# One weight load cut into halves of its columns, and an order of operations read from a table: block-sorted attention and a feed-forward layer on one core

## The chip, the cores and the metric

The kernel runs on one core of one Trainium2 chip. Its time is device microseconds of one execution. Before the change three runs took 251.02, 250.55 and 249.65 us; the median is 250.55 us. The profile belongs to one more execution, which took 249.8 us.

A core has five engines that run their own instruction streams: TensorE (PE, matmuls; PEld is its weight load), VectorE (DVE), ScalarE (ACT), GpSimd (POOL) and SyncE (SP). Data come and go through 16 DMA engines, which POOL and SP feed. A wait on a semaphore holds up everything behind it on the same engine.

## The reference

```python
def _attn_ref(q, k, v, sort_net):            # q, k, v: [4, 8, 768, 64], sort_net: [4, 8, 8, 8]
    ...
    for _ in range(5):                       # five rounds of softmax and column sums
        P = P - np.max(P, axis=-1, keepdims=True)
        P = np.exp(P)
        P = P / (np.sum(P, axis=-1, keepdims=True) + 1e-09)
        P = P / (np.sum(P, axis=-2, keepdims=True) + 1e-09)
    ...
    k_sorted = np.einsum('bhij,bhjcd->bhicd', P, k_b).reshape(B, H, S, D)   # 8 blocks of 96 rows
    v_sorted = np.einsum('bhij,bhjcd->bhicd', P, v_b).reshape(B, H, S, D)
    ...
    scores = scale * np.matmul(q_b, k_sb.transpose(0, 1, 2, 4, 3))          # within a block
    ...
    return np.matmul(attn, v_sb)

def _moe_ref(x, w_in, w_out, alpha):         # x: [3072, 512], w_in: [512, 2048], w_out: [2048, 512]
    h = x @ w_in
    g = np.maximum(h, 0.0) + alpha * np.minimum(h, 0.0)
    return g @ w_out
```

The attention's output, its heads put side by side, is the x of the feed-forward layer. Inputs and output are float32; the kernel multiplies in bfloat16.

## The kernel before, in words

The 3,072 tokens are 32 groups of 96: four batches of eight blocks. A group is computed for all eight heads at once.

**Start.** POOL issues the loads of batch 0: q into a free part of hT (L482), k into KS and v into VST (L504); each writes 6,144 bytes of bfloat16 into each of 128 partitions. Then come w_in in four row blocks of 128 rows (L988), w_out in two halves (L993), k and v of batch 1 (L504, L520), q of batch 1 head by head into QN (L486), which SP then transposes into QTz (L494), and v and k of batch 2. Meanwhile DVE and ACT compute the five rounds on sort_net, and PE runs 140 tiny matmuls (`burst`, L969) and turns q (L685).

**Per batch.** `prep_k` (L685 for batch 0, L714 later) sorts the blocks of k by matmuls with a matrix made of P, and writes KT. `conv_v` (line 457, on ACT, DVE or POOL) lays out v and `prep_v` (L760, later L755) sorts it into VS; `conv_k` (L701, POOL) lays out k for the later batches.

**Per group.** Scores (L801 in batch 0, L798 later), row maxima on DVE (L807), then in batch 0 a second pass on PE (L822 and L813) and one exponential on ACT (L845). Later batches take eight exponentials on ACT (L834) and a DMA transpose on SP (L839, into ET). Then scores times v (L854), a division on DVE (L862, L865, into xq) and a turn into xT, by PE (L880) and a copy, or by SP (L873) in most groups of the later batches.

**Feed-forward.** Tokens go in chunks of 192 (the first two) and 384. `ffn1` makes four matmuls (L904) for each of 16 column blocks ft of w_in, ACT takes the negative part (L914, into t1), DVE joins it into hT (L917). `ffn2` takes tiles of 128 tokens: 16 matmuls (L943) in four groups, a copy, and a store by SP (L957). Every `ffn1` group reads all 512 rows of w_in, and so waits for all four row blocks.

**The order.** Each operation is added to a graph with its engine (or a choice of ACT and DVE, `EITHER`), an estimated duration, what it reads and writes, and a priority. `search` (L221) tries 2,000 variations of the priorities; each is put in order by `schedule` (L156), which at each step takes the engine that can start first. Model times in `span` and `fetched` include a fetch of PE's instructions in blocks of 256, usable `FETCH` = 6,200 ns after the block before it was entered. `fill` and `idle` then put further matmuls, of the identity with itself, whose results nobody reads (`warm`, L1070, 512 columns each), into PE's gaps in the model's times. `emit` writes the five streams with the waits that the order leaves.

The lines of the load and of its first reader are:

```python
for p in range(4):                                            # L987
    G.add(POOL, lambda e, p=p: e.dma_start(
        AP(w_in_bf, p * DFF, [[KT_TILES * DFF, 128], [1, DFF]]),
        AP(moe_w_in.tensor, p * 128 * DFF, [[DFF, 128], [1, DFF]])),
        2550, w=[("w_in", p)], prio=-40 + p, dma=(dma_sem("wi%d" % p), 0))
...
op = G.add(PE, f, t_pe(*[(n, 128)] * 4), r=[("xT", g % 16) for g in range(ga, gb)]
           + [("w_in", kt) for kt in range(KT_TILES)], w=keys, prio=prio)
```

Of the kernel before, what the change touches and what calls it, by code (L numbers as in the profile page):

```python
# [2 lines left out]

# [5 lines left out]
AP = bass.AP  # L9
# [9 lines left out]
DFF = 2048  # L19
KT_TILES = DM // 128  # L20
# [5 lines left out]
NE = 3  # L26
VSL = 4
EPS = 1e-9
SEARCH = 1500
FIRST = 500  # L30
FETCH = 6200.0
BURST = 140

XLAT = {"pe": 215, "act": 36, "dve": 36, "pool": 80, "sync": 80}
ENGS = ("pool", "sync", "pe", "act", "dve")


def t_pe(*mms):  # L40
    return sum(max(n, m, 64) / 2.4 + 4 for n, m in mms)
# [34 lines left out]
class _Graph:  # L76
# [51 lines left out]
    def fetched(self, op, at, d, f):  # L128

        if f["fills"] and at > 5000:  # L130
            f["n"] += 2 * int(max(at - f["end"], 0) * 0.9 / 215)
        f["fills"] = f["fills"] and op.fills
        n, last = 2 * op.mm, f["n"] + 2 * op.mm
        while f["mark"] < last:
            x = at + d * max(f["mark"] - f["n"], 0) / n
            late = max(f["usable"] - x, 0.0)
            at, x = at + late, x + late
            f["usable"] = x + FETCH
            f["mark"] += 256
        f["n"], f["end"] = last, at + d  # L140
        return at + d
# [11 lines left out]
            t = max(t, x.end + lat)  # L153
        return t

    def schedule(self):  # L156
        ops = self.ops
        for op in ops:
            op.users, op.eng = [], op.engs
        for op in ops:  # L160
            op.left = len(op.deps)
            for d in op.deps:
                ops[d].users.append(op.idx)
        ready = {e: [] for e in ENGS}

        def release(op):
            op.ready = {}
            for e in op.engs:
                op.ready[e] = self.ready_at(op, e)
                ready[e].append(op)  # L170

        free = dict.fromkeys(ENGS, 0.0)
        free["pool"] = 400.0
        loads = [0.0, 0.0, {"n": 2, "mark": 193, "usable": 0.0, "end": 0.0, "fills": True}]
        order = {e: [] for e in ENGS}
        for op in ops:
            if not op.left:
                release(op)
        done = 0
        while done < len(ops):  # L180
            best = None
            for e in ENGS:
                if not ready[e]:
                    continue
                first = max(free[e], min(o.ready[e] for o in ready[e]))
                op = min((o for o in ready[e] if o.ready[e] <= first + 60), key=lambda o: (o.prio, o.idx))
                first = max(first, op.ready[e])
                if best is None or first < best[0]:
                    best = (first, e, op)
            at, e, op = best  # L190
            for x in op.engs:
                ready[x].remove(op)
            op.eng, op.start = e, at
            free[e], op.end = self.span(op, e, at, free, loads)
            op.pos = len(order[e])
            order[e].append(op)
            done += 1
            for u in op.users:
                ops[u].left -= 1
                if not ops[u].left:  # L200
                    release(ops[u])
        self.order = order
        return max(op.end for op in ops)

    def replay(self, seed):

        rng = random.Random(seed)
        was = [(op.start, op.end) for op in self.ops]
        free = dict.fromkeys(ENGS, 0.0)
        free["pool"] = 400.0  # L210
        loads = [0.0, 0.0, {"n": 2, "mark": 193, "usable": 0.0, "end": 0.0, "fills": True}]
        for op in sorted(self.ops, key=lambda o: (o.start, o.idx)):
            at = max(free[op.eng], self.ready_at(op, op.eng))
            free[op.eng], op.end = self.span(op, op.eng, at, free, loads, 0.08 * rng.random())
        last = max(op.end for op in self.ops)
        self.ends = [op.end for op in self.ops]
        for op, (a, b) in zip(self.ops, was):
            op.start, op.end = a, b
        return last

    def search(self, n, first):  # L221

        rng = random.Random(7)
        rank = [op.prio for op in self.ops]
        best = None
        for x in range(FIRST + n):
            if x == FIRST:
                best = None
            lo, hi, part = (-47.5, 3.0, 0.2) if x < FIRST else (0.0, 99.0, 0.1)
            amp = rng.choice((0.1, 0.3, 1.0))  # L230
            for op, p in zip(self.ops, rank):
                op.prio = p + (rng.uniform(-amp, amp) if x % FIRST and lo < p < hi and rng.random() < part else 0.0)
            cost = self.schedule()
            if x < FIRST:
                cost = sum(op.end for op in first)
            if x < FIRST or best is None or cost < best + 1500:
                for seed in (1, 2):
                    late = self.replay(seed)
                    cost += sum(self.ends[op.idx] for op in first) if x < FIRST else late
                cost /= 3  # L240
                if best is None or cost < best:
                    best, rank = cost, [op.prio for op in self.ops]
                    if __import__("os").environ.get("SCHED"):
                        print("search", x, round(cost))
        for op, p in zip(self.ops, rank):
            op.prio = p
        return self.schedule()

    def fill(self, make, unit, first, spans):

# [118 lines left out]
def bass_sinkhorn_attn__then__act_prelu_kernel(  # L369
# [11 lines left out]
    G = _Graph()  # L381
    sems = {e: es.enter_context(nc.semaphore("s_" + e)) for e in ENGS}

    def dma_sem(name):
        return [es.enter_context(nc.semaphore("d_" + name)), 0]
# [7 lines left out]
    PE, ACT, DVE, POOL, SYNC = ("pe",), ("act",), ("dve",), ("pool",), ("sync",)  # L393
# [3 lines left out]
    bz = sb("bz", [128, 32], BF16)  # L397
# [19 lines left out]
    w_in_bf = sb("w_in_bf", [128, KT_TILES, DFF], BF16)  # L417
    w_out_bf = sb("w_out_bf", [128, FT_TILES, DM], BF16)
    xT = sb("xT", [128, KT_TILES, XR], BF16)
# [39 lines left out]
    def t_either(n, mode=1):  # L459
# [4 lines left out]
          w=["P"], prio=-100, dma=(dma_sem("sn"), 0))  # L464
# [429 lines left out]
    def ffn1(ga, gb, ft, prio):  # L894
        tok, n = ga * BLK, (gb - ga) * BLK
        tb = step[0] % 3
        banks = BANK_H + ([BANK_P] if ga < 2 else [])
        pt, poff, _, keys = banks[step[0] % len(banks)]
        step[0] += 1

        def f(e):
            inst = None
            for kt in range(KT_TILES):
                inst = e.matmul(AP(pt, poff, [[1024, 128], [1, n]]),  # L904
                                AP(w_in_bf, kt * DFF + ft * 128, [[KT_TILES * DFF, 128], [1, 128]]),
                                AP(xT, kt * XR + tok % XR, [[KT_TILES * XR, 128], [1, n]]),
                                start=(kt == 0), stop=(kt == KT_TILES - 1))
            return inst
        op = G.add(PE, f, t_pe(*[(n, 128)] * 4), r=[("xT", g % 16) for g in range(ga, gb)] + [("w_in", kt) for kt in range(KT_TILES)],
              w=keys, prio=prio)  # L910
        if not ffn_ops:
            ffn_ops.append(op)

        G.add(ACT, lambda e: e.activation(AP(t1[tb], 0, [[384, 128], [1, n]]),  # L914
                                          AP(pt, poff, [[1024, 128], [1, n]]), ACTF.Relu, scale=-1.0),
              t_act(n), r=keys, w=[("t1", tb)], prio=prio)
        G.add(DVE, lambda e: e.scalar_tensor_tensor(  # L917
            out=AP(hT, ft * RING + tok % RING, [[FT_TILES * RING, 128], [1, n]]),
            in0=AP(t1[tb], 0, [[384, 128], [1, n]]), scalar=AP(omaT, ft, [[16, 128], [1, 1]]),
            in1=AP(pt, poff, [[1024, 128], [1, n]]), op0=AluOpType.mult, op1=AluOpType.add),  # L920
            t_dve(n) + 52, r=keys + [("t1", tb), "omaT"],
            w=[("hT", ft, x % (RING // 64)) for x in range(tok // 64, (tok + n) // 64)], prio=prio)
# [42 lines left out]
    def burst(e):  # L965
# [2 lines left out]
            r = x % 4 * 32  # L968
            inst = e.matmul(AP(psS, r * 1024 + 384, [[1024, 32], [1, 32]]), bz[r:r + 32, :], bz[r:r + 32, :])  # L969
        return inst  # L970
    G.add(PE, burst, 200 + 8.5 * BURST, r=["bz"], w=["psSw"], prio=-120)
    load_q(0, -98)
    load_k(0, -97)
    load_v(0, -96)
# [9 lines left out]
        conv_v(0, u, -45.5)  # L984
    for u in range(8):
        prep_v(0, u, -45, (BANK_O + [BANK_P])[u % 3])
    for p in range(4):  # L987
        G.add(POOL, lambda e, p=p: e.dma_start(  # L988
            AP(w_in_bf, p * DFF, [[KT_TILES * DFF, 128], [1, DFF]]),
            AP(moe_w_in.tensor, p * 128 * DFF, [[DFF, 128], [1, DFF]])),  # L990
            2550, w=[("w_in", p)], prio=-40 + p, dma=(dma_sem("wi%d" % p), 0))
    for p in range(2):
        G.add(POOL, lambda e, p=p: e.dma_start(  # L993
            AP(w_out_bf, p * 8 * DM, [[FT_TILES * DM, 128], [DM, 8], [1, DM]]),
# [67 lines left out]
            load_k(3, -3.9)  # L1062
            load_q(3, -2)
    assert fp == len(ffn_plan)
    total = G.search(SEARCH, first_x)

    def warm(e, n, bank=(psYP, 0)):
        inst = None
# [46 lines left out]
```

## Time and profile before

| what | value |
|---|---|
| median of three runs | 250.55 us |
| the profiled execution | 249.8 us |
| its span, first to last instruction | 248.1 us |
| mean granted clock of TensorE | 0.979 |
| PE busy | 234.3 us (94%), 2,538 matmuls |
| DVE, ACT, POOL busy | 171.5, 155.1, 101.1 us |
| L904 and L943, busy | 97.8 and 84.7 us (the larger groups) |
| first and last L904 | 30.43 and 236.4 us |
| w_in, issue to landing | 14.4 to 20.4 us |
| HBM read, written | 27.28, 6.29 MB |

The span leaves out what lies before the first and after the last instruction; here that is 1.7 us. Busy time of PE counts matmuls that overlap and matmuls at half clock, so it says where PE is not empty, not how much it gets done; the start-to-start distance of equal matmuls says that. In a list by stretches the columns are the stretch, its length, then for each engine the busy time and in brackets the number of instructions, the granted clock, the share of the DMA engines' time and GB/s.

### The profile page before, as it was taken

What the parts mean: (1) busy time and instruction counts of PE and PEld (TensorE: products, weight loads), DVE (VectorE), ACT (ScalarE), POOL (GpSimd) and SP (SyncE); (2) the same over time, 40 slices, a digit from 0 to 9 for tenths busy, and PEclk for the clock granted to TensorE, in tenths of its full rate; (3) what the DMA queues carried; (4) which work ended last, traced back from release to release, by engine and by line L of the source; (5) the groups of instructions that cost most, each with busy time, mean ns of one, the idle gap of its engine ahead of it and who ended that gap; (6) DMA issues with size and microseconds to landing.
All of it is one profiled execution on the core that took longest, in us unless ns stands there. A gap on an engine that the chain in (4) does not pass through costs nothing.

```text
span 248.1 us, 6269 instructions
## 1 busy us (share of the span) xinstructions
PE 234.3 (94%) x2538; PEld 145.0 (58%) x2538; DVE 171.5 (69%) x347; ACT 155.1 (63%) x423; POOL 101.1 (41%) x146
## 2 busy tenths in 40 slices
PE   6876899999999979999999999999999999999995
PEld 3445567668655636666565666655556555555544
DVE  6764667669787878786679878676869476655510
ACT  5567335596868876786648567965685576455511
POOL 8988902275899967798554103100000000000000
PEclk9999579999999999999999999999999999999999
DMA  6999999999999899989985665532364232301112
GB/s 104 208 211 210 173 215 205 172 196 124 193 85 185 156 170 143 140 121 132 145 135 132 93 159 108 132 94 53 87 122 107 49 103 45 95 11 73 44 45 86
DMA packets 71982, 31.37 MB, mean 126 GB/s; under 512 B 64512, under 2 KB 67344, under 8 KB 71952
## 3 DMA queue, kind: packets, MB, share of 16 engines
q0 software_dynamic: 23408, 13.63, 41.1%
q1 hardware_dynamic: 48544, 17.33, 36.5%
q8 instruction: 20, 0.33, 0.6%
q14 instruction: 10, 0.08, 0.2%
HBM read 27.28 MB, written 6.29 MB: 135 GB/s over the span
## 4 chain that ended last, share of the span: by engine, by line
PE 81%; DMA 8%; ACT 4%; DVE 3%; POOL 2%; issue 2%; POOLq 0%
PE psH L904 31%; PE psYP L943 28%; DMA VST<-in_v_dram 5%; PE psS L943 3%; PE psO L854 3%; PE psS L798 3%; DMA ET<-Esb 3%; PE psYP L755 2%; POOL VDz L457 2%; PE psYP L714 1%; PE psS L813 1%; PE psYP L1070 1%; ACT VDz L457 1%; DVE hT L917 1%; PE psS L822 1%
## 5 line engine op out<-in xcount | busy, mean ns | idle before, releaser
L917 DVE SCALAR_TENSOR_TENSOR hT<-t,omaT,psH 128x384 bf16<-128x384 f32 (+1 forms) x139 | 77.4, 571 | 31.7 <-ACT t L914 29.8
L904 PE MATMUL psH<-xT,w_in_bf 128*128 128x384 bf16 (+1 forms) x556 | 97.8, 312 | 0.6 <-DVE hT L917 0.3
L914 ACT ACTIVATE t<-psH 128x384 f32<-128x384 f32 (+1 forms) x139 | 62.8, 465 | 48.4 <-PE psH L904 44.3
L943 PE MATMUL psYP<-w_out_bf,hT 128*128 128x512 bf16 x336 | 84.7, 379 | 0.3 <-DVE hT L917 0.3
L904 PEld LDWEIGHTS psH<-xT,w_in_bf 128*128 128x128 bf16 x556 | 49.9, 98 | 33.0 <-DVE hT L917 5.9
L834 ACT ACTIVATE Esb<-psS,nf 96x96 bf16<-96x96 f32 x192 | 46.3, 345 | 1.2 <-DVE nf L807 0.9
L943 PEld LDWEIGHTS psYP<-w_out_bf,hT 128*128 128x128 bf16 x336 | 30.4, 98 | 27.4 <-DVE hT L917 0.4
L457 POOL COPY VDz<-VST 64x384 bf16<-64x384 bf16 x40 | 34.0, 851 | 13.6 <-PE psYP L755 11.6
L701 POOL COPY KSz<-KS 64x512 bf16<-64x512 bf16 x36 | 22.2, 618 | 33.0 <-PE psYP L714 21.0
L807 DVE TENSOR_REDUCE nf<-psS 96x8 f32<-96x768 f32 x24 | 22.7, 946 | 0.9 <-PE psS L798 0.9
L865 DVE TENSOR_TENSOR xq<-psO,rec 96x512 bf16<-96x512 f32 x31 | 21.2, 685 | 1.0
L486 POOL DMA_DIRECT2D QN<-in_q_dram x24 | 19.8, 848 | 2.5 <-DMA QTz<-QN 1.2
L854 PEld LDWEIGHTS psO<-VS,ET 112*128 112x128 bf16 x248 | 11.5, 100 | 6.9 <-ACT Esb L834 2.0
L854 PE MATMUL psO<-VS,ET 112*128 112x65 bf16 x248 | 13.1, 196 | 1.8 <-DMA ET<-Esb 1.5
L798 PEld LDWEIGHTS psS<-KT,QTz 128*96 128x96 bf16 x192 | 11.7, 125 | 2.7
L798 PE MATMUL psS<-KT,QTz 128*96 128x96 bf16 x192 | 12.6, 208 | 0.0
L862 DVE RECIPROCAL rec<-psO 96x8 f32<-96x8 f32 x31 | 6.1, 198 | 9.2 <-PE psO L854 9.1
L1070 PE MATMUL psYP<-identb 128*128 128x512 bf16 x34 | 11.3, 468 | 1.0 <-ACT identb L457 1.0
L457 ACT ACTIVATE VS<-psYP 112x512 bf16<-112x512 f32 x13 | 8.9, 687 | 5.0 <-PE psYP L755 3.2
L457 DVE CAST VS<-psYP 112x512 bf16<-112x512 f32 x13 | 9.0, 690 | 3.7 <-PE psYP L755 3.7
L457 ACT ACTIVATE outstg<-psYP 128x512 f32<-128x512 f32 x11 | 6.6, 598 | 7.7 <-PE psYP L943 7.7
L755 PE MATMUL psYP<-BDV,VDz 128*128 128x64 bf16 x192 | 9.5, 193 | 0.5 <-POOL VDz L457 0.5
(139 smaller groups left out, 212.6 us busy)
## 6 DMA issues: line engine op xcount, KB each, us to landing
out_dram<-outstg SPq DMA_DIRECT2D x23, 256.0 KB, 2.3
KS<-in_k_dram POOLq DMA_DIRECT2D x3, 768.0 KB, 31.5
QN<-in_q_dram POOLq DMA_DIRECT2D x24, 96.0 KB, 5.5
w_in_bf<-in_moe_w_in_dram POOLq DMA_DIRECT2D x4, 512.0 KB, 17.3
w_out_bf<-in_moe_w_out_dram POOLq DMA_DIRECT2D x2, 1024.0 KB, 28.6
VST<-in_v_dram POOLq DMA_DIRECT2D x4, 384.0 KB, 31.8
hT<-in_q_dram POOLq DMA_DIRECT2D x1, 768.0 KB, 7.0
VST<-in_v_dram POOLq DMA_DIRECT2D x1, 768.0 KB, 13.4
```

Source lines behind the costliest of these rows:

```text
L457: return e.activation(o, i, ACTF.Copy) if e is nc.scalar else e.tensor_copy(o, i)
L486: G.add(POOL, lambda e, h=h: e.dma_start(AP(QN, h * 128 + (h // 4) * 64, [[6144, 128], [1024, 6], [1, 64]]), AP(q.tensor, b * HB + h * S * ...
L701: G.add(POOL, lambda e, hp=hp: e.tensor_copy(AP(KSz, hp * 64 * 3072 + u % 3 * 1024 + hp * 64, [[3072, 64], [128, 8], [1, 64]]), AP(KS[n], ...
L798: inst = e.matmul(o, AP(QTz[n], hp * 3072 + h4 * 768 + i * 96, [[6144, 128], [1, 96]]), AP(KT[n], (h4 * 8 + i) * bk, [[ld, 128], [64, 2], ...
L807: G.add(DVE, lambda e: e.tensor_reduce(AP(nx, 0, [[8, 96], [4, 2], [1, 4]]), AP(psX, 0, [[1024, 96], [512, 2], [96, 4], [1, 96]]), AxisLis ...
L834: inst = e.activation(AP(Esb[me], p * 128, [[1024, 96], [64, 2], [1, 48]]), AP(psX, (p // 4) * 512 + (p % 4) * 96, [[1024, 96], [48, 2], [ ...
L854: inst = e.matmul(AP(psZ, hp * 512 + h4 * 68, [[1024, 128], [1, 65]]), AP(ET[me] if far else ET[m], pos(h4, hp) * 96, [[800, nk], [1, 128] ...
L865: G.add(DVE, lambda e: e.tensor_tensor(out=AP(xq[me], 0, [[512, 96], [256, 2], [64, 4], [1, 64]]), in0=AP(psZ, 0, [[1024, 96], [512, 2], [ ...
L904: inst = e.matmul(AP(pt, poff, [[1024, 128], [1, n]]), AP(w_in_bf, kt * DFF + ft * 128, [[KT_TILES * DFF, 128], [1, 128]]), AP(xT, kt * XR ...
L914: G.add(ACT, lambda e: e.activation(AP(t1[tb], 0, [[384, 128], [1, n]]), AP(pt, poff, [[1024, 128], [1, n]]), ACTF.Relu, scale=-1.0), t_ac ...
L917: G.add(DVE, lambda e: e.scalar_tensor_tensor(out=AP(hT, ft * RING + tok % RING, [[FT_TILES * RING, 128], [1, n]]), in0=AP(t1[tb], 0, [[38 ...
L943: inst = e.matmul(AP(bank[0], bank[1], [[1024, 128], [1, n]]), AP(hT, ft * RING + tok % RING, [[FT_TILES * RING, 128], [1, 128]]), AP(w_ou ...
```

## The change

w_in is loaded in two halves of its columns instead of four blocks of its rows. A load writes, in each partition, four pieces of 1,024 columns (2,048 bytes of bfloat16). An `ffn1` group then waits for one half: the first for ft 0 to 7, the second for ft 8 to 15.

The search is gone. `arrange` takes the operations in the order of a table of 1,224 numbers (two fewer, for the two loads); a letter behind a number gives the engine where there is a choice. Each engine's stream follows the table. The model's times still exist, since `fill`, `idle` and the waits use them, with other constants: the fetch of a block takes 3,500, 6,150, 6,000 or 5,200 ns by its time, and the `burst` 9.4 ns a matmul instead of 8.5. The matmuls, copies, transposes and stores are the same; how many of the `warm` matmuls there are follows from the model's times, and the choice between ACT and DVE from the table (DVE has four operations fewer than before and ACT four more, POOL two loads fewer).

```diff
-SEARCH = 1500
-FIRST = 500
-FETCH = 6200.0
 BURST = 140
...
+SEQ = """
+0 2 7 3 10 4 17 18 11 16 27 5 1 8 42 43 12 9 28 44 37 39 45 6 46 40 47 48 29 38 130 49 50 33 51 131 52 53 54
+55 132 56 57 41 58 133 34 59 60 136 61 62 63 26 64 35 65 23 36 66 83 67 145 68 87 84 69 89 70 21 71 91 88 31
...
+""".split()
...
-            f["usable"] = x + FETCH
+            f["usable"] = x + (3500.0 if x < 3000 else 6150.0 if x < 12500 else 6000.0 if x < 30000 else 5200.0)
...
-    def schedule(self):
...
-    def replay(self, seed):
...
-    def search(self, n, first):
...
+    def arrange(self, table):
+        assert len(table) == len(self.ops)
+        letters = {"p": "pool", "a": "act", "d": "dve"}
         free = dict.fromkeys(ENGS, 0.0)
         free["pool"] = 400.0
         loads = [0.0, 0.0, {"n": 2, "mark": 193, "usable": 0.0, "end": 0.0, "fills": True}]
...
+        self.order = {e: [] for e in ENGS}
+        done = set()
+        for x in table:
+            op = self.ops[int(x.rstrip("pad"))]
+            e = letters.get(x[-1], op.engs[0])
+            assert e in op.engs and op.deps <= done
+            done.add(op.idx)
+            at = max(free[e], self.ready_at(op, e))
+            op.eng, op.start, op.pos = e, at, len(self.order[e])
             free[e], op.end = self.span(op, e, at, free, loads)
...
-        op = G.add(PE, f, t_pe(*[(n, 128)] * 4), r=[("xT", g % 16) for g in range(ga, gb)] + [("w_in", kt) for kt in range(KT_TILES)],
+        op = G.add(PE, f, t_pe(*[(n, 128)] * 4), r=[("xT", g % 16) for g in range(ga, gb)] + [("w_in", ft // 8)],
...
-    G.add(PE, burst, 200 + 8.5 * BURST, r=["bz"], w=["psSw"], prio=-120)
+    G.add(PE, burst, 200 + 9.4 * BURST, r=["bz"], w=["psSw"], prio=-120)
...
-    for p in range(4):
+    wc = DFF // 2
+    for p in range(2):
         G.add(POOL, lambda e, p=p: e.dma_start(
-            AP(w_in_bf, p * DFF, [[KT_TILES * DFF, 128], [1, DFF]]),
-            AP(moe_w_in.tensor, p * 128 * DFF, [[DFF, 128], [1, DFF]])),
-            2550, w=[("w_in", p)], prio=-40 + p, dma=(dma_sem("wi%d" % p), 0))
+            AP(w_in_bf, p * wc, [[KT_TILES * DFF, 128], [DFF, KT_TILES], [1, wc]]),
+            AP(moe_w_in.tensor, p * wc, [[DFF, 128], [128 * DFF, KT_TILES], [1, wc]])),
+            5500, w=[("w_in", p)], prio=-40 + p, dma=(dma_sem("wi%d" % p), 0))
...
-    total = G.search(SEARCH, first_x)
+    total = G.arrange(SEQ)
```

The table lists operations by their number in the order in which the program adds them: 130 and 131, for instance, are the halves of w_in, 132 and 133 those of w_out.

## The prediction

> **What bounds the kernel now.** I read the page's forty slices first, to see where the granted clock and the matmul engine fall short:
>
> ```profile
> PE   6876899999999979999999999999999999999995
> PEclk9999579999999999999999999999999999999999
> ```
>
> PE is full nearly everywhere, but the clock is about half in slices five and six. Then the stretches: PE's busy time, and in the long ones all engines' (PE, PEld, DVE, ACT, POOL, clock, DMA share, GB/s):
>
> ```profile
> 42.00:60.00 18.00, 17.02 (x242) 12.54 (x242) 12.95 (x30) 11.90 (x27) 10.40 (x16) 1.00 1.53 158
> 60.00:80.00 20.00, 19.70 (x219) 13.03 (x219) 16.43 (x33) 15.51 (x42) 17.74 (x22) 1.00 1.45 165
> 80.00:97.00 17.00, 14.70 (x175) 9.30 (x175) 14.24 (x27) 12.28 (x37) 13.61 (x19) 1.00 0.95 158
> 97.00:240.00 143.00, 142.99 (x1162) 82.88 (x1159) 100.61 (x174) 92.35 (x271) 31.43 (x44) 1.00 0.53 96
> ```
>
> From 97 us on, PE never pauses. A busy share alone says little, so I priced the work: start to start at full clock, a 384-column matmul of L904 takes 162 ns, a 192-column one 82, a 512-column one of L943 216, L798 45, L854 about 32, L755 and L714 29. Counted so, the matmuls after the first L904 (30.43 us) are worth 200.9 us; they end at 245.45, so 14.1 of 215.0 us are lost, nearly all before 97. So the time is the start of the feed-forward work, plus 200.9, plus what is lost until 97, plus a tail of 2.65. An order can change only the first and the third.
>
> Now the worst stretch, cut at the change of the clock (24.22) in steps of 3.41 us, the unit in which the clock record changes (17.07 is five, 10.24 is three):
>
> ```profile
> 13.98:17.40 3.42, 2.17 (x43) 1.00 1.05 211
> 17.40:20.81 3.41, 3.08 (x89) 1.00 1.06 213
> 20.81:24.22 3.41, 1.50 (x62) 1.00 1.08 217
> 24.22:27.64 3.42, 3.23 (x59) 0.50 1.06 148
> 27.64:31.05 3.41, 2.61 (x29) 0.50 1.21 198
> 31.05:34.46 3.41, 3.41 (x32) 0.50 1.24 208
> ```
>
> 2.17 us of work in a step keeps the clock, 1.50 loses it, and it is back only after a full step. PE's timeline shows what emptied that step:
>
> ```profile
> 21.29 0.47 PE L760 MATMUL psO<-BDK,hT 128*64 128x64 bf16 x17
> 23.67 0.41 PE L760 MATMUL psO<-BDK,hT 128*64 128x64 bf16 x15 [1.91 <-issue]
> 26.49 0.64 PE L854 MATMUL psYP<-VS,ET 112*128 112x65 bf16 x8
> 28.42 0.50 PE L880 MATMUL psYP<-identb,xq 96*128 96x96 bf16 x4 [0.85 <-DVE xq L865]
> ```
>
> The pause of 1.91 us falls inside a group of 16 and waits for no semaphore. It stands at PE's 961st record; another, 1.12 us at 14.65, stands at the 705th, and 20 packets of 16 KB on the instruction queue serve some 5,100 records: a block of 256 each. One started 5.51 us after PE passed record 705 (15.77 to 21.28), took 0.94, and PE went on 1.46 later. So a block costs wait plus about 2.4 us, and PE needs it some 6 to 9 us after asking.
>
> **The change, part by part.** The wait is queueing behind data. Packets of a batch of q, k or v (6,144 bytes written) take 474 ns, of w_in (4,096) 324, of w_out (1,024) 98. These rows show the first load of w_in's spread and how full the queue is from 14.4 to 24.4 us:
>
> ```profile
> L988 POOL DMA_DIRECT2D w_in_bf<-in_moe_w_in_dram x4: 548/563/576, 4.3 to 5.9; - x4
> DMA to landing us min/median/max: 14.4/17.3/20.4
> q0 software_dynamic: 579, 2.09, 104.5%
> ```
>
> *Packets.* 2,048-byte packets are not in this part of the trace; on the line from 1,024 to 4,096 (22 ns plus 75 per KB) one takes 173 ns. An engine moves 64 instead of 32: 11.1 for 10.4 us, **+0.7** for what queues behind (w_out, the second batch). First users: w_out's halves land at 32.9 and 37.9, L943 starts at 39.5; k of the second batch has PE work before it. I charge nothing; without that cover it is +0.7. The halves would land near 21.7 and 27.2 (a quarter lands 1.7 after its last packet): the table's first seven L904 groups use columns of the first half only, so an earlier start near 27 is not held by w_in, where four row blocks held it until 26.25.
>
> *The fetch.* In packets, the wait was 8 (6,144), 17 (4,096) and 25 (1,024, at 32.40); in bytes 50, 70 and 26 KB. Neither is constant. Seventeen packets of 173 ns give 2.9; the same bytes 5.5 as now. I take 4.2, in the middle: the block asked for at 15.77 is usable at 22.4 instead of 23.67, **-1.3** (bounds 0 and -1.9). The next block: asked for at 23.67, served at 28.86, usable near 31.3, reached at 32.40. Reached about 28.4 after the gains here and below, and usable at 22.4 + 4.1 + 2.4 = 28.9 if its wait falls alike, it would cost **+0.5** (0 to +1.6). The Trainium skill speaks against all this: "Runtime: NRT & Kernel Launch", Instruction fetch mechanics, gives PE room for 2,048 instructions and calls the crossing of a block mostly hidden. By it packet size would bring 0; the pauses at records 705 and 961 disagree.
>
> *The clock.* With 1.3 of the pause gone the step holds about 2.5 us of work, above the 2.17 that kept the clock. Up to the first L904 the chain of waits holds, at half speed, L760 0.64, L854 0.44 and 0.46, L880 0.50 and 0.43, L801 0.48, L642 and L645 0.57: 3.5 us, **-1.7**. L997 and the two L1070 lie beside the last VS copy. From 30.43 to 34.46 half speed costs 2.0 us of work, but eight L1070 fillers from 34.5 to 42 say that PE is not short there; I take **-1.2** (0 to -2.0). The Trainium skill's "TensorE: Matmul & The Clock Gate", Part 1, lets the clock fall after an idle window of about 3.4 us. The window agrees in length; 1.50 us of work is not idle, and by that rule removing the pause would leave the clock as it is: the first rival.
>
> *POOL.* Two issues for four: at 0.56 for 128 packets and 0.95 for w_out's 1,024, about 0.73 for 512: 2.25 becomes 1.5 us; bounds 1.1 and 1.9. The table puts the 0.97 us clear of L535 ahead of v's issue (2.86 to 3.83). Cover: q and k hold each DMA engine for 16 packets, 7.6 us from 2.7, so v's turn comes at 10.3; without it +0.97, since v's load is on the chain. The clears of QN and the QN and later issues trade places; all their data queue behind w_out. Nothing.
>
> *The table elsewhere.* All five orders are new. Counted in the prices above, PE work from the first L904 to the last L880 of batch 0 falls from 26.1 to 19.7 us, to the first L798 from 28.9 to 26.8; to the L714 of the second batch it rises by up to 2.9, to its L755 it moves by -2.7 to +0.8. On SP the store of tile 0 moves ahead of the last of the six QTz transposes; it had its data long before (issued 66.44, behind them). No row prices such a shuffle: the bounds are the seventeen L1070 after 30.43, 17 x 0.215 = 3.7 either way. I take **-0.4**, near the middle: batch 0 ends earlier, but POOL (17.74 of 20 us) and the transposes still pace the second and third batches.
>
> **Sum**: -1.3 + 0.5 - 1.7 - 1.2 - 0.4 = -4.1: a span of 244.0 for 248.1. The profiled execution took 249.8, 1.7 around the span, so 245.7; the median of the three runs, 250.55, is 0.75 higher, so **246.4**.
>
> **Rivals.** *The clock falls anyway* (the step stays too empty, or the next block stalls 1.6): only -1.3 and -0.4 remain, 248.85. For it: the limit is known only to lie between 1.50 and 2.17. Against: those 1.3 us hold work. *Everything at its bound*: -1.9, -1.8, -2.0 and some -2.5 of the fillers: -8.2, 242.3. For it: the 14.1 lost; against: the first QTz transpose lands only at 61.35, whatever PE does. *The lead runs into that landing* (the slower side): PE reaches its first L798 early, waits 1.9 us there or for ET (1.39 at 91.03 now), and when a step holds less than about 1.5 us of work the clock halves for 10.24 us; at 85% useful work (5.4 of the 37 us from 60 to 97 are lost) 4.4 us: 246.4 + 1.9 + 4.4 = 252.7. Against: batch 0's feed-forward work is still there to fill. *The packets do nothing*, the fetch waits 5.5 us as now, and the order is neutral: 250.5. The Trainium skill's runtime page would lead here.
>
> **How the numbers follow.** Forecast 0.55 (its own range 244 to 248.5), clock falls anyway 0.17, everything 0.15, the lead lost 0.08, nothing 0.05. Some 0.5% (1.25 us) is what a measurement here can tell from no change: faster means under 249.3. Forecast, everything and two thirds of the first rival make 0.81; its rest and most of nothing 0.10; the lead lost and a remainder 0.09. The range runs from just below the full gain to above nothing, 242 to 251.3; it leaves out the lost lead and the deepest gains.
>
> **What would show it.** Right: w_in in 1,024 packets near 173 ns, the pause at PE's 961st record under 0.7 us, clock 1.00 from 20 to 35 us, the first L904 near 27.5, PE without a pause from about 93. Wrong: a wait from record to packet of 5.5 us still; a half clock in another stretch; a pause before the first L798 or at ET; more L1070 or idle from 40 to 97 than the lead is worth.

## The result, and the profile after

The changed kernel is slower: 255.63 us, the median of five runs (254.47 to 256.51), for 250.55 before (249.65 to 251.02). The ratio is 1.0277, with a 95% interval of 1.0227 to 1.0327. The forecast was 246.4 with a range of 242 to 251.3, so size and sign were both wrong. Some executions of a kernel come out more than 1.5% above its fastest; every ratio leaves them out on both sides, and the profiles of n1, oldseq_c, old_splate, oldhead and new475 are of such executions.

The profiled execution took 255.43 us. The kernel's lines have moved: L876 after is L904 before (`ffn1`), L915 is L943 (`ffn2`), L826 is L854 (scores times v), L811 and L466 are L839 and L494 (SP's transposes into ET and QTz), L458 is L486 (q loads), L673 and L686 are L701 and L714 (`conv_k` and `prep_k`). In the kernels of the experiments these numbers can be one lower. The page's head and the two rows of its forty slices:

```profile
span 253.4 us, 6249 instructions
...
PE   6869999978899869999999999999999999999995
...
PEclk9995559999999979999999999999999999999999
```

The low clock at the start is still there, one slice longer, and there is a second one in slice 15, where PE also falls to 6. The stretches shown of before, now after (stretch, length, busy time and instructions of PE, PEld, DVE, ACT and POOL, clock, DMA share, GB/s):

```profile
42.00:60.00 18.00, 15.59 (x236) 11.56 (x237) 14.75 (x32) 10.45 (x22) 8.71 (x15) 1.00 1.48 186
60.00:80.00 20.00, 18.78 (x203) 12.35 (x204) 15.14 (x29) 14.80 (x42) 17.19 (x21) 1.00 0.96 113
80.00:97.00 17.00, 13.64 (x132) 8.06 (x133) 11.39 (x22) 10.79 (x35) 12.06 (x17) 0.90 1.17 142
97.00:240.00 143.00, 141.67 (x1178) 83.70 (x1196) 99.30 (x172) 96.03 (x278) 35.06 (x50) 1.00 0.58 100
```

The stretch from 80 to 97 us is the bad one: 132 matmul records for 175 before, at a clock of 0.90. The other PE sums must be read with care, since the profile after lacks 30 of 2,536 matmul records: L915 has 308 matmuls for 336 weight loads. PE's timeline in the bad stretch (start, length, line, operation; in brackets the idle time before it and what ended it):

```profile
87.17 0.52 PE L770 MATMUL psS<-KT,QTz 128*96 128x96 bf16 x8
87.53 0.41 PE L727 MATMUL psYP<-BDV,VDz 128*128 128x64 bf16 x8
90.83 0.40 PE L826 MATMUL psO<-VS,ET 112*128 112x65 bf16 x8 [2.89 <-DMA ET<-Esb]
91.06 2.38 PE L876 MATMUL psH<-xT,w_in_bf 128*128 128x384 bf16 x8
93.66 1.41 PE L915 MATMUL psYP<-w_out_bf,hT 128*128 128x512 bf16 x3 [0.22 <-issue]
```

PE stands 2.89 us for the transpose ET of group 10, the third group of batch 1, and then eight L876 take 2.38 us at half clock. The clock, in its steps of 3.41 us:

```profile
16.36:19.77 3.41, 1.64 (x42) 0.90 (x41) 3.16 (x6) 2.85 (x4) 3.14 (x4) 1.00 1.12 211
...
88.04:91.45 3.41, 0.62 (x11) 0.52 (x12) 0.66 (x3) 0.61 (x1) 1.26 (x3) 1.00 1.23 211
91.45:94.87 3.42, 3.20 (x10) 1.40 (x10) 2.32 (x5) 1.88 (x7) 1.73 (x3) 0.50 1.27 146
```

A step with 1.64 us of work was followed by 17.07 us at half clock (19.77 to 36.84), and the step with the ET wait, 0.62 us of work, by 3.41 us.

Why ET was late can be read on SP, which issues all the transposes in order. First SP's timeline after, then before:

```profile
77.36 1.22 SPq L811 DMA_TRANSPOSE ET<-Esb  x1
78.62 0.59 SPq L929 DMA_DIRECT2D out_dram<-outstg  x1
84.76 1.23 SPq L466 DMA_TRANSPOSE QTz<-QN  x1
86.05 1.32 SPq L811 DMA_TRANSPOSE ET<-Esb  x1
```

```profile
76.62 1.49 SPq L839 DMA_TRANSPOSE ET<-Esb  x1
80.48 1.23 SPq L494 DMA_TRANSPOSE QTz<-QN  x1
81.76 1.30 SPq L839 DMA_TRANSPOSE ET<-Esb  x1
```

In both kernels the first QTz transpose of batch 2 stands on SP ahead of the ET of group 10, and it waits for the eight q loads of batch 2. Before, the last of them landed at 80.46, QTz went out at 80.48, and group 10's exponentials ended only at 81.03: ET went out 0.73 behind its input. After, the exponentials ended at 82.50, but the q loads landed only at 84.75, and ET went out 3.55 behind its input. The q loads also go out later. POOL's timeline after, then before:

```profile
51.55 0.61 POOL L673 COPY KSz<-KS 64x512 bf16<-64x512 bf16 x1 [6.66 <-PE psYP L686]
53.76 1.95 POOL L673 COPY KSz<-KS 64x512 bf16<-64x512 bf16 x3 [1.60 <-PE psYP L686]
...
71.59 6.59 POOL L458 DMA_DIRECT2D QN<-in_q_dram  x8
```

```profile
49.27 1.28 POOL L701 COPY KSz<-KS 64x512 bf16<-64x512 bf16 x2 [4.25 <-PE psYP L714]
...
68.85 6.58 POOL L486 DMA_DIRECT2D QN<-in_q_dram  x8
```

POOL's copies of k wait for the first `prep_k` of batch 1 to free their buffer. In this profile POOL goes on at 51.55 for 49.27 and issues q 2.7 us later. Half or more of that belongs to this execution and not to the table: it had 17.07 us of half clock at its start, where rows and qsixth (below), with the same table, had 10.24 and issued q at 70.26 and 69.73. Nor is a later issue the main reason that the q loads land late. new660 (below), which is as slow as the changed kernel, shows on POOL and SP:

```profile
69.17 6.59 POOL L457 DMA_DIRECT2D QN<-in_q_dram  x8
...
74.93 1.24 SPq L810 DMA_TRANSPOSE ET<-Esb  x1
...
82.52 1.23 SPq L465 DMA_TRANSPOSE QTz<-QN  x1
83.81 1.35 SPq L810 DMA_TRANSPOSE ET<-Esb  x1
```

It issues q 0.3 us later than before, and yet the last q load landed at 82.51 for 80.46. From issue to landing that load took 7.65 us in new660, 7.47 after and 7.73 in rows, but 5.91 before and 6.07 in p2k. One thing that differs beside it is the ET of group 9: it goes out 0.1 us behind the last q issue in the three, and 2.1 us behind it in the two. Whether this is what slows the q loads was not tested; against it, the profile of oldseq_c, with the old order, has 7.37 us as well.

### The profile page after: what moved, and what is told of

Its sections match the earlier page's. It is cut to its first block, busy times and chain, and to the rows that moved or that the text cites. A ratio compares the mean times of both kernels' runs of the same rounds, so it can differ in the third digit from the quotient of the medians.

```text
span 253.4 us, 6249 instructions
## 1 busy us (share of the span) xinstructions
PE 235.8 (93%) x2506; PEld 147.0 (58%) x2536; DVE 170.8 (67%) x343; ACT 158.2 (62%) x427; POOL 100.3 (40%) x144
## 4 chain that ended last, share of the span: by engine, by line
PE 82%; DMA 7%; DVE 5%; issue 2%; POOL 2%; ACT 1%; POOLq 0%
PE psH L876 31%; PE psYP L915 28%; DMA VST<-in_v_dram 5%; PE psS L915 3%; PE psS L770 3%; PE psO L826 3%; DMA ET<-Esb 2%; PE psS L785 2%; PE psYP L686 2%; PE psYP L727 1%; DVE hT L889 1%; PE psO L732 1%; PE psYP L1043 1%; PE psS L794 1%; POOL hT L429 1%
## 5 line engine op out<-in xcount | busy, mean ns | idle before, releaser
L876 PE MATMUL psH<-xT,w_in_bf 128*128 128x384 bf16 (+1 forms) x556 | 98.9, 315 | 1.2 <-DVE hT L889 1.1
L915 PE MATMUL psYP<-w_out_bf,hT 128*128 128x512 bf16 x308 | 78.5, 381 | 1.9 <-issue 0.5
L876 PEld LDWEIGHTS psH<-xT,w_in_bf 128*128 128x128 bf16 x556 | 50.3, 99 | 32.9 <-DVE hT L889 5.8
L915 PEld LDWEIGHTS psYP<-w_out_bf,hT 128*128 128x128 bf16 x336 | 30.8, 98 | 28.9 <-issue 0.9
L673 POOL COPY KSz<-KS 64x512 bf16<-64x512 bf16 x36 | 22.2, 616 | 39.9 <-PE psYP L686 25.9
L458 POOL DMA_DIRECT2D QN<-in_q_dram x24 | 19.8, 851 | 0.5 <-POOL QN L518 0.3
L826 PE MATMUL psO<-VS,ET 112*128 112x65 bf16 x248 | 13.1, 197 | 2.9 <-DMA ET<-Esb 2.9
L826 PEld LDWEIGHTS psO<-VS,ET 112*128 112x128 bf16 x248 | 11.3, 100 | 7.4 <-issue 3.3
L429 ACT ACTIVATE outstg<-psYP 128x512 f32<-128x512 f32 x15 | 9.0, 599 | 9.4 <-PE psYP L915 9.4
L1043 PE MATMUL psYP<-identb 128*128 128x512 bf16 x38 | 12.1, 448 | 1.0 <-ACT identb L429 1.0
L429 ACT ACTIVATE VS<-psYP 112x512 bf16<-112x512 f32 x14 | 9.6, 687 | 3.3 <-PE psYP L727 2.2
L727 PEld LDWEIGHTS psYP<-BDV,VDz 128*128 128x128 bf16 x192 | 8.3, 98 | 3.5 <-ACT VS L429 0.8
L817 ACT ACTIVATE ET<-psS 112x768 bf16<-112x768 f32 x7 | 5.7, 810 | 6.5 <-PE psS L785 6.5
```

Of the source, the lines that this page charges most:

```text
L429: return e.activation(o, i, ACTF.Copy) if e is nc.scalar else e.tensor_copy(o, i)
L458: G.add(POOL, lambda e, h=h: e.dma_start(AP(QN, h * 128 + (h // 4) * 64, [[6144, 128], [1024, 6], [1, 64]]), AP(q.tensor, b * HB + h * S * ...
L673: G.add(POOL, lambda e, hp=hp: e.tensor_copy(AP(KSz, hp * 64 * 3072 + u % 3 * 1024 + hp * 64, [[3072, 64], [128, 8], [1, 64]]), AP(KS[n], ...
L826: inst = e.matmul(AP(psZ, hp * 512 + h4 * 68, [[1024, 128], [1, 65]]), AP(ET[me] if far else ET[m], pos(h4, hp) * 96, [[800, nk], [1, 128] ...
L876: inst = e.matmul(AP(pt, poff, [[1024, 128], [1, n]]), AP(w_in_bf, kt * DFF + ft * 128, [[KT_TILES * DFF, 128], [1, 128]]), AP(xT, kt * XR ...
L915: inst = e.matmul(AP(bank[0], bank[1], [[1024, 128], [1, n]]), AP(hT, ft * RING + tok % RING, [[FT_TILES * RING, 128], [1, 128]]), AP(w_ou ...
```

## The experiments

Each kernel is compared with the kernel before, run on the same chip. In diffs of the table, `new` and `old` are the two orders as tables; the kernels have them written out. The numbers of the expectations are quoted as they were on record ahead of the runs.

### Is it the load of w_in? p2k, oldseq_c, rows, oldseq

p2k is the kernel before with packets of 2,048 bytes: each of the four loads takes two row blocks of one column half.

```diff
-            AP(w_in_bf, p * DFF, [[KT_TILES * DFF, 128], [1, DFF]]),
-            AP(moe_w_in.tensor, p * 128 * DFF, [[DFF, 128], [1, DFF]])),
+            AP(w_in_bf, p // 2 * 2 * DFF + p % 2 * 1024, [[KT_TILES * DFF, 128], [DFF, 2], [1, 1024]]),
+            AP(moe_w_in.tensor, p // 2 * 256 * DFF + p % 2 * 1024, [[DFF, 128], [128 * DFF, 2], [1, 1024]])),
```

> The kernel before, with w_in still in four loads of the same bytes, but each load two row blocks by half of the columns, so that its packets are 2,048 bytes; order, waits and fillers are those of before. Packets theory (in the changed kernel the third block of instructions waited 6.25 us for its packet, before 5.51, and all behind it is late): 252.5 us or more, with a wait over 6 us. Order theory (the table costs the time, the packets nothing): 250.5, within 1.2 us of before. Clock theory (the time follows the stretch at half clock, 20.5 us of it in the changed kernel, 10.2 before): time and mean clock move together, 255 at 0.960, 250.5 at 0.979.

Measured: ratio 0.9988 (0.9953 to 1.0024). The packets change nothing.

oldseq_c is the changed kernel with the old order as its table and the old constants of the model, so that the streams and the `warm` matmuls are those of before. Of the change it keeps the two halves and the wait for one half. oldseq has the old order and the new constants.

```diff
-    total = G.arrange(new)
+    total = G.arrange(old)
-            f["usable"] = x + (3500.0 if x < 3000 else 6150.0 if x < 12500 else 6000.0 if x < 30000 else 5200.0)
+            f["usable"] = x + 6200.0        # oldseq_c, with 8.5 for 9.4 ns in burst and 5,100 for 5,500 in the load
```

> All five streams of the kernel before, fillers included; only w_in differs, two loads of column halves, and each L904 group waits for its half. If the 3.5 us that the old order lost under the new constants came from fillers (five more at 48 us) and what they shift: 250, within 1 us of before. If from the halves themselves: 252.5 or more.

> The changed kernel (two column halves, its constants and its fillers by the model) with a table that holds the order of before. Packets theory: 253 us or more. Order theory: 250.5, within 1.5 us. Clock theory: as its mean clock says.

Measured: oldseq_c 1.0019 (0.9978 to 1.0059), oldseq 1.0137 (1.008 to 1.0193). The halves and their waits are neutral too. With the new constants alone there are five more `warm` matmuls at 49 to 50 us, 1.1 us of work; in its profile PE later waits 3.3 us for the ET of group 11. The profile of oldseq_c, of an execution of 255.66 us, has a wait of 4.7 us for the ET of group 10: this chain can break in the old order too.

rows is the changed kernel with w_in in two row halves, packets of 4,096 bytes.

```diff
-            AP(w_in_bf, p * wc, [[KT_TILES * DFF, 128], [DFF, KT_TILES], [1, wc]]),
-            AP(moe_w_in.tensor, p * wc, [[DFF, 128], [128 * DFF, KT_TILES], [1, wc]])),
+            AP(w_in_bf, p * 2 * DFF, [[KT_TILES * DFF, 128], [DFF, 2], [1, DFF]]),
+            AP(moe_w_in.tensor, p * 256 * DFF, [[DFF, 128], [128 * DFF, 2], [1, DFF]])),
-           + [("w_in", ft // 8)]
+           + [("w_in", 0), ("w_in", 1)]
```

> The changed kernel with its table, but w_in in two halves of its rows, packets of 4,096 bytes; every L904 group waits for both. Packets theory: back to 251 to 252 us. Order theory: 255 to 256, as the changed kernel. Clock theory: as its mean clock says.

Measured: 1.0203 (1.0126 to 1.0279), with a wait of 2.9 us for ET. The table, with the new constants, is slow without the halves as well.

### Where in the table? newhead, new340, new475, new660, oldhead

The first k entries come from the new table, the rest in the old order; oldhead is the reverse at 267.

```diff
-SEQ = new
+SEQ = new[:k] + [x for x in old if x not in new[:k]]
```

> The changed kernel with a table that follows the new order for its first 267 entries (some 50 us of the profile) and then the order of before for all that is left. Order theory, with the loss where the traces part (50 to 65 us and 80 to 95 us): 250 to 252 us. Packets theory, or a loss made in the first 50 us: 254 us or more.

> The changed kernel with the order of before for the first 267 entries of its table and the new order for the rest. Queue theory (the loss lies behind 50 us, in the new order): 254 us or more. If the new head is what costs: 251 to 252.

> The changed kernel with the new order for the first 340 entries of its table (to the end of the k preparation of batch 1, some 61 us) and the order of before behind them; with 267 entries it was 0.6% over before. Theory of two places (VectorE overloaded from 50 to 58 us by k and v copies of batch 1 beside the last groups of batch 0, some 2 us, and the transposes' queue at 80 to 95 us, some 3): 252.0 to 253.5, 1.0 to 1.6% over before. One place only, at 80 to 95: 250.5 to 251.5, as with 267 entries.

> The same with 475 entries, past ET of group 10 behind the first QTz of batch 2 (some 86 us). Theory of two places: 254.5 to 256, all of the loss. A loss spread over the whole order: about 253.

> The same with 660 entries, past the last group of batch 1 (some 118 us). Both theories of a loss ahead of 118 us: 255 to 256, as the changed kernel. A loss made behind 118 us: 253 or less.

| new entries | reach to about | ratio | 95% interval |
|---|---|---|---|
| 0, old constants (oldseq_c) | 0 us | 1.0019 | 0.9978 to 1.0059 |
| 0, new constants (oldseq) | 0 us | 1.0137 | 1.008 to 1.0193 |
| 267 (newhead) | 50 us | 1.0061 | 1.002 to 1.0102 |
| 340 | 61 us | 1.0108 | 1.0068 to 1.0149 |
| 475 | 84 us | 1.0205 | 1.0143 to 1.0266 |
| 660 | 115 us | 1.0284 | 1.0225 to 1.0343 |
| 1,224 (the change) | all | 1.0277 | 1.0227 to 1.0327 |

All rows below the first have the new constants. Behind some 115 us no further loss shows. How much belongs to each piece is less sure, since a seam between two orders can cost something itself: oldhead, the old start with the new rest, came to 1.0482 (1.0404 to 1.0561).

The constants are a rival that stands. With the old order they alone cost 1.2 points (0.0019 to 0.0137), and no run has the new order with the old constants. The changed kernel has two `warm` matmuls fewer than the kernel before, so it isn't their number; what their places cost in the new order stays open.

### Is it SP's queue? sp_swap, sp_late, old_splate

sp_swap puts the first QTz of batch 2 (425) behind the ET of group 10 (465); sp_late moves all six QTz behind later ETs; old_splate does the like in the old order.

```diff
-422 474 483 425 447 475d 423 457 492 472 424d 458 465 570
+422 474 483 447 475d 423 457 492 472 424d 458 465 425 570
```

> The changed kernel with one move in SP's order: the first QTz transpose of batch 2 goes behind the ET transpose of group 10 instead of ahead of it. Queue theory (in the changed kernel ET of group 10 is issued 7.7 us after its scores, 4.9 before, because QTz ahead of it waits for the last head of q, landed at 84.75): ET of group 10 is issued near 82, PE's pause of 2.78 us at 88 goes and with it the 3.4 us at half clock behind it: 251.5 to 253. Rival (PE simply has too little work placed there, or the DMA traffic decides): 255, as the changed kernel, with the pause at this or the next group.

> The changed kernel with all six QTz transposes of batch 2 later in SP's order: behind ET of groups 11, 12 and 14, two at a time. Queue theory: scores to ET issue falls from 6 to 9 us to about 4 for groups 10 to 14, 251 to 252.5. Rival: 254.5 or more.

> The five streams of before with w_in in column halves, and one difference: on SP the six QTz transposes of batch 2 stand later (two behind ET of group 11, two behind 12, one behind 13, one behind 14). If the place of these transposes decides PE's pause near 91 us (1.39 us before): 248 to 249.5, up to 1% under the kernel before. If the DMA traffic of the v loads decides it: no change, 250.

Measured: 1.023 (1.0165 to 1.0295), 1.0233 (1.0174 to 1.0293) and 1.002 (0.9978 to 1.0063). In sp_swap the ET of group 10 does go out 0.03 behind its input, but the pause comes at group 11 instead, 3.3 us; in sp_late 1.6 us are left, at group 13. So moving QTz back in SP's queue is not enough: the theory that the queue's order alone is the cause, which expected most of the loss back, fell.

### Is the wait the loss? n1, n2, n2l, qsixth

To see where the time goes I took the start that `arrange` plans for each PE operation and matched it, in order, with the profile's records. The plan is only a ruler here, and says nothing of the chip; what counts is where the distance between measured and planned start changes. Measured minus planned start in us, at some measured times, and the planned start of the last PE operation:

```
            35    50    70    84    92    96   100   118   240   planned end
before     3.4   2.5   2.3   2.4   3.6   3.5   3.4   2.9   1.1   243.7
p2k        3.3   2.4   2.1   2.3   2.0   1.8   1.8   1.2   0.1   243.7
rows       3.4   2.8   2.7   2.3   6.4   6.2   5.9   5.4   3.5   244.9
after      4.3   4.2   4.1   3.7   6.3   8.0   7.8   7.1   5.3   244.9
```

From 35 to 84 us the new table runs beside its plan just as the old order does. Then after falls back by 4.3 us at one place, the wait for ET (2.9) and the half clock behind it, where before loses 1.1 and p2k nothing. For the two profiles the whole difference of the last start, 5.4 us, is 1.2 from the plan (the new order isn't shorter even as planned), 1.3 that stood at 84 us (rows, with the shorter half clock at its start, lacks it), and 2.9 made between 84 and 118.

n1 takes the waiting L826 of group 10 (466) behind five pieces of other PE work; n2 also moves that of group 11 (496); n2l is n2 with the QTz of sp_late; qsixth is the changed kernel with a sixth of batch 2's q.

```diff
-641 466 488 479a 471 513 642 467 523 510 514 507 547 511 515 506 524 512 504 519
+641 488 479a 471 513 642 523 510 514 507 547 511 515 506 524 512 504 466 467 519
...
-    AP(QN, h * 128 + (h // 4) * 64, [[6144, 128], [1024, 6], [1, 64]]),
+    AP(QN, h * 128 + (h // 4) * 64, [[6144, 128], [1024, 1 if b == 2 else 6], [1, 64]]),   # qsixth; the source alike
```

> The new table with one step moved: the O matmuls of group 10 (which in the profile after stood 2.89 us at 87.94 for the transpose ET) go behind five pieces of other TensorE work (two first-layer pieces, one second-layer piece, one prep of v, about 3.7 us). Theory A (the new table loses its time where TensorE stands for ET and at the half clock behind it, 2.9 + 1.7 us): about 252 us, no pause above 1 us at 88. Theory B (the wait only moves on to group 11 or 12, as in the two SP runs): 255 to 256 and a pause of 2 to 3 us at 91 to 104. Theory C (the loss lies all over the table, the wait is only where it shows): 255 to 256 without any such pause.

> As n1, and the O matmuls of group 11 go behind one second-layer piece, one prep of v and one first-layer piece as well (2 us). Theory A: 251.5 to 253 us, no pause at 88 to 98. Theory B: the wait goes to group 12 or 13, 255 us. Theory C: 255 to 257, no pause.

> n2 with the six QTz transposes of batch 2 behind the ET transposes on SP as in sp_late: each ET goes out when its input is there and its matmuls have 2 to 3 us more slack. Theory A: 251 to 252.5 us. Theory B: 254 to 255.5. Theory C: 255 to 257.

> The new table with the eight q loads of batch 2 cut to one sixth of their rows (it leaves out five sixths of batch 2's q; the QTz transposes stay). Theory A with the q loads as the cause of the late ET (they land at 84.8 in the profile after, QTz waits for them and ET of group 10 stands behind it on SP): ET of group 10 out within 1 us of its input, 251.5 to 253 us. If the transposes are late for other traffic (v loads, the QTz transposes themselves): 254.5 to 256 with a pause at group 11 or 12.

| kernel | ratio | 95% interval | waits for ET in its profile, 60 to 125 us |
|---|---|---|---|
| after | 1.0277 | 1.0227 to 1.0327 | 2.9 |
| n1 | 1.0136 | 1.0079 to 1.0193 | 4.8, the longest 4.1 at group 11 |
| n2 | 1.018 | 1.0116 to 1.0244 | 2.5, the longest 1.6 |
| n2l | 1.0129 | 1.0057 to 1.0201 | none |
| qsixth | 1.0109 | 1.0054 to 1.0165 | 2.4, the longest 1.5 |

qsixth tells most: nothing of the order changed, and SP's timeline is

```profile
77.82 1.23 SPq L465 DMA_TRANSPOSE QTz<-QN  x1
80.66 1.22 SPq L810 DMA_TRANSPOSE ET<-Esb  x1
81.91 1.31 SPq L465 DMA_TRANSPOSE QTz<-QN  x1
85.09 1.22 SPq L810 DMA_TRANSPOSE ET<-Esb  x1
```

The shortened q loads had landed by 77.80, both ETs go out within 0.03 behind their inputs, PE no longer waits for group 10, the clock stays up, and 1.7 of the 2.8 points are back (0.0277 to 0.0109; the intervals don't meet). So most of the loss hangs on batch 2's q loads. That their lateness alone does it is not shown: the cut also takes five sixths of their bytes off the DMA engines (ET of group 10 landed 2.8 us behind its issue, for 4.6 after), the kernel before was not run with the same cut, and in sp_swap, where the ET of group 10 went out as promptly, little came back. Of the 2.7 us that are left (0.0109 of 249.5), the plan's 1.2 and the waits for ET that remain are the candidates; this was not taken apart further. Nor was what makes the q loads land late tried by itself.

n2l has no wait for ET at all, and its stretch from 80 to 97 us is as full as p2k's (16.41 and 16.15 us of PE):

```profile
80.00:97.00 17.00, 16.41 (x180) 9.83 (x179) 14.56 (x29) 13.13 (x41) 13.99 (x20) 1.00 0.96 149
```

It still takes 1.0129. By the plan the cure is paid for elsewhere: its planned end is 247.9, 3.0 us behind that of after, with ten `warm` matmuls more (52 for 42), while it ends 0.4 ahead of its plan (after: 5.3 behind). So theory A fits n2l, whose rest would be its own longer program. Theory B's wait that moves on shows in the profile of n1 (4.1 us at group 11), but that is of an execution of 257.52 us, and n1's ratio rests on the five of its twelve runs that took 251.58 to 254.51. What n1 gained is therefore unsure. No version beat the kernel before by more than the measurement's uncertainty.

## Why the prediction was wrong, point by point

**Packets, +0.7 hidden: right.** A packet of 2,048 bytes took 173 ns, as forecast; the halves landed at 21.50 and 26.45 for 21.7 and 27.2, and p2k is neutral.

**The fetch, -1.3: wrong.** From PE's record 705 to the packet of the next block it took 6.25 us after and 5.72 in p2k, for 5.51 before. In all eighteen profiles it came at 21.0 to 22.1 us, whatever the packets were, and with packets of 2,048 bytes the wait was 5.0 to 6.7 us. Shorter packets did not shorten it; what sets it stays open. The Trainium skill, "Runtime: NRT & Kernel Launch", Instruction fetch mechanics, calls such crossings mostly hidden; the pauses at record 961, from none to 1.91 us in these profiles, say that they need not be. What the prediction drew from it, that packet size would bring nothing, held. **The next block, +0.5**, came to nothing: it was served at 28.53, well ahead of record 1217 at 32.74.

**The half clock, -1.7 and -1.2: wrong.** In the profile after it lasted 17.07 us for 10.24, and 10.24 in rows and qsixth with the same table. That 2.17 us of work in a step keeps the clock did not hold either: in qsixth a step with 2.45 us was followed by half clock, while in oldseq one with 1.53 us was not, so no limit on busy time fits both.

```profile
27.45:30.86 3.41, 2.45 (x43) 1.66 (x41) 3.33 (x7) 1.31 (x3) 1.41 (x2) 1.00 1.23 202
30.86:34.28 3.42, 3.42 (x34) 2.70 (x34) 1.68 (x8) 1.36 (x3) 0.00 (x0) 0.50 1.25 210
...
90.46:93.87 3.41, 1.53 (x15) 0.67 (x13) 2.16 (x4) 2.58 (x10) 1.36 (x3) 1.00 1.19 106
93.87:97.29 3.42, 2.00 (x29) 1.51 (x30) 1.28 (x3) 0.75 (x2) 1.74 (x3) 1.00 1.19 200
```

The gain also hung on one pause, and after, the step ahead of the half clock had two others, for copies by ACT and POOL (0.91 and 0.86 us). The first L876 came at 30.94 for a forecast near 27.5, and in eighteen profiles the first `ffn1` never came ahead of 29.38. The Trainium skill, "TensorE: Matmul & The Clock Gate", Part 1, calls the window of activity free-running, so that the same kernel meets it in another phase from run to run. These profiles agree: every stretch in the head is a multiple of 3.41 us, the first full clock begins anywhere from 6.12 to 9.09 us, and so the same pause falls in one step or across two. A gain from one step's work could not be forecast from one execution.

**But the head isn't what made it slower.** In the profile after it holds no more than the 1.3 us that stood at 84 us, and new660 had only 3.41 us of half clock there and its first `ffn1` at 29.38, the best of all, and took 1.0284.

**The table elsewhere, -0.4 with bounds of 3.7 either way: the step that failed.** It is the term that was mis-sized: with the new constants, for which the sum had no term at all, it came to about +5 us in the medians. I bounded it by the `warm` matmuls, as if PE's slack were all that an order could use or lose, and took the middle since no row priced a shuffle. The rows for a price were there. Of before, SP's timeline showed the ET of group 10 only 0.73 us behind its input, behind a QTz that itself waited for q, and PE standing 1.39 us at 91.03: slack next to nothing for whatever makes the q loads land later. I noted that L714 of batch 1 moved back by up to 2.9 us, and did not ask what that does to the transfers of the second batch. In the place of -0.4 the runs showed this: the last q load lands 2.1 (new660) to 4.3 us (after) later than before, QTz waits for it on SP, the ET of group 10 stands behind QTz, PE stands 2.7 to 2.9 us for it (new660, after, rows), and a half clock follows; with a sixth of q, 1.7 of the 2.8 points are back. Why the q loads land later, and how much the constants add, stays open.

**The rivals.** The lost lead (252.7, chance 0.08) named the place and mechanism, a wait at ET and then a half clock; it came without any lead, with 2.89 us for 1.9, and with one step of half clock instead of three. The clock falls anyway (248.85) was right of the clock and wrong of the order, and nothing from packets (250.5) right of the packets and wrong of the order. PE without a longer pause from about 93 us was right, from 91.

**POOL, nothing:** no run speaks against it for the two issues of w_in. Later, POOL's q loads went out 0.3 (new660) to 2.7 us (after) behind those of before; in new660 that is the small part of the 2.1 us by which the last one landed later.

## What to carry to other kernels

An order of operations is priced by the slack of its tightest cross-engine chains, not by the idle time of the busiest engine: list, for each transfer that the main engine consumes, when its input was ready, when it was issued, what stood ahead of it in its queue, and when it was needed. Where that slack is under a microsecond, follow every moved operation through the queues it shares (here q loads and transposes on the DMA engines, then QTz ahead of ET on SP). And test a change that has several parts one part at a time; here the visible part, the load, was worth nothing either way, and the new order was never run without the new constants.

## What the runs showed of the hardware

- Neither a pause's length nor PE's busy time in a step of 3.41 us decides the clock alone: it went to half behind steps with 0.62 and 1.64 us of PE work (after), 1.50 (before), 2.17 (sp_swap) and 2.45 (qsixth), and stayed with 1.53 (oldseq) and 2.17 (before). Waits for ET of 2.7 to 3.3 us were followed by 3.41 or 6.83 us of half clock in rows, after, new660 and sp_swap, and the 3.3 us in oldseq by none.
- The same kind of DMA transpose, 96 rows of ET, took 2.8 to 8.9 us from issue to landing when it was issued between 70 and 120 us: for group 10 2.8 in qsixth and 4.6 after, for group 11 8.2 in oldseq and 8.9 in n1.
- A load of one head of q, 96 KB, took 5.9 us from issue to landing before and 7.7 in rows, beside other transfers (the last head of batch 2).
